# The first two token tiles of an MLP in k order, weight rows as they come, and a column sum by DMA transpose: one core of a Trainium2 chip

## The chip, the cores and the metric

The kernel runs on one core of a Trainium2 chip as one launch. The metric is the time of one execution on the device in microseconds (us); the median of the runs is compared. A profile of one execution shows when each instruction of each engine ran: TensorE (PE, with its weight loads PEld), VectorE (DVE), ScalarE (ACT), GpSimd (POOL) and the DMA queues that SyncE (SP) and ScalarE issue on.

## The reference

A linear-attention block and an MLP read the same layernormed input, and both are added to x. All tensors are bfloat16; the sequence has 2048 tokens, D = 640, F = 1536, and there are 32 heads of 20.

```python
xn = layernorm(x)                               # over D, eps 1e-5
# A: linear attention
q, k, v = split(xn @ wqkv)                      # 32 heads of 20
phi = lambda t: where(t > 0, t + 1, exp(t)) + 1e-6
pq, pk = phi(q), phi(k)
kv  = einsum("bhsd,bhse->bhde", pk, v)
z   = einsum("bhsd->bhd", pk)                   # the sum of pk over all tokens
num = einsum("bhqd,bhde->bhqe", pq, kv)
den = einsum("bhqd,bhd->bhq", pq, z)[..., None] + 1e-6
A = (num / den) @ wo
# B: the MLP
B = gelu(xn @ w1 + b1) @ w2 + b2
out = x + A + B
```

## The kernel before

Nothing is scheduled by a planner's costs: `Planner` only records what the program text calls for, one in-order list for each engine, and adds the semaphore waits that reads and writes of named resources need. The order on each engine is the order of the calls. An instruction group that ends in a mark increments its engine's semaphore once.

The 2048 tokens are 16 tiles of 128. x is loaded by tiles on SP's queue (`dma_x`), W1 in four quarters of 384 of its 1536 columns (`dma_w1`), between the loads of x: x0, x1, W1 quarters 0 and 1, x2, x3, quarter 2, x4 and x5, quarter 3, x6 and x7. x8 to x15 are issued later, in `ln_rest`. While the first data is under way, TensorE runs filler matmuls on constants.

A tile's layernorm is two `bn_stats` on VectorE (`ln_half`, halves of 320 columns), an aggregate, a power on GpSimd for the reciprocal deviation (`ln_aggr`), and one subtract and multiply on VectorE (`ln_norm`). The normalised tile must be transposed so that D lies on the partitions. Tiles 0 and 1 are transposed on TensorE into two PSUM banks (`transp2`, L331) and copied out by ScalarE (384 columns) and VectorE (256) in `copy2` (L339, L340); tile 2 on TensorE into one bank (`transp`, L374; `xnT_copy`, L382); all others by DMA transposes on SP's queue (`xnT_dma`, L263).

The first MLP matmul (`h_unit`, L393) takes one block of 128 of the 1536 hidden columns and n tiles of tokens: five matmuls, one for each 128 rows k of W1, sum in one PSUM bank, and ScalarE's GELU (L397) writes the result to HG. PSUM has 8 banks, handed out in a ring (`take`). A block needs its whole quarter of W1 and all five k of its tiles. The list `plan` sets TensorE's order: blocks of tile 0, `"T1"` (transposes of tile 1), more blocks of tiles 0 and 1 alone and together, `"T2"` (transposes of tile 2), then ever wider groups: 128, 256, 384 and at last 512 tokens a matmul.

After the MLP's first half come the keys (L502, L508, phi by ScalarE's exp at L490 and VectorE's L491 and L493), then G = xn^T pk (`g_group`, L535; `g_rem`, L544), while VectorE sums pk over the tokens (`z_sums`: 15 additions, L555 and L558, then a split into a high and a low bfloat16 part, L561 and L564). Then the queries (`q_chunk`, L588, with the same phi) in four chunks of five units. Between chunk 0 and chunk 1 stand `z_step` (L570: ten matmuls with a column of ones, one column each, which finish z; L574 copies it and L576 makes ZB) and `kvt_step` (L598, L605). The denominators (`den_mm`, L652) need ZB and all queries. The second MLP half and the attention's output (L709, L720) end the kernel. In the queues, SP carries every load, the DMA transposes and part of the stores; ScalarE's queue carries b1, the spread reciprocals and the other stores.

## Time and profile before

| | |
|---|---|
| median of 3 runs | 206.49 us (206.47 to 206.69) |
| the profiled execution: own time, span | 206.66 us, 204.9 us |
| TensorE busy | 201.3 us (98%), 1227 matmuls |
| VectorE, ScalarE, GpSimd busy | 108.2, 73.2, 34.0 us |
| first MLP matmul, first key matmul | 6.59 us, 59.65 us |
| moved by DMA | 21.37 MB, of it 13.08 MB read from HBM |

All times inside the profile count from the start of its span; the own time of that execution is longer by what lies around the span. A group's row gives the line, the engine, what it writes and reads, and how often; its length is that of one instruction alone, and matmuls are pipelined, so the distance between starts is shorter than the length. In the timeline, brackets give the idle time before an instruction and what ended it.

### The profile page before, as it was taken

The page shows a single profiled execution, that of the slowest core. Times are in us where ns is not written, and L with a number is a line of the kernel's source. Part 1 is how long each engine was busy: PE and PEld are TensorE (multiplying, and loading weights), DVE is VectorE, ACT ScalarE, POOL GpSimd, SP SyncE. Part 2 cuts the span into 40 slices and gives each one's busy share as a digit, 9 for nine tenths or more (in the row PEclk, how much of TensorE's full clock was granted, in tenths as well). Part 3 has the DMA queues.
Part 4 walks back from the last instruction along what each step waited for, and adds up shares of the span by engine and source line. Part 5 has one row for each costly group of instructions (what it writes and reads, how often), then busy time and mean ns, then how long its engine had stood idle before and what let it go on. Part 6 is the DMA issues. An engine that isn't in the chain of part 4 may idle for free.

```text
span 204.9 us, 3306 instructions
## 1 busy us (share of the span) xinstructions
PE 201.3 (98%) x1227; PEld 104.2 (51%) x1227; DVE 108.2 (53%) x236; ACT 73.2 (36%) x142; POOL 34.0 (17%) x85
## 2 busy tenths in 40 slices
PE   8999999999999999999999999999999999999995
...
GB/s 152 349 174 116 202 136 118 87 362 316 374 85 3 26 26 26 26 3 0 0 32 5 0 0 12 95 46 190 318 215 114 133 89 54 51 26 51 78 29 51
DMA packets 36217, 21.37 MB, mean 104 GB/s; under 512 B 21352, under 2 KB 36200, under 8 KB 36200
## 3 DMA queue, kind: packets, MB, share of 16 engines
...
q14 instruction: 7, 0.06, 0.1%
HBM read 13.08 MB, written 2.62 MB: 77 GB/s over the span
## 4 chain that ended last, share of the span: by engine, by line
PE 95%; DMA 3%; SPq 1%; DVE 0%; issue 0%
PE ps L709 29%; PE ps L393 25%; PE ps L588 11%; PE ps L502 8%; PE ps L535 8%; PE ps L720 7%; DMA W<-in_B_w_dram 3%; PE ps L544 2%; PE ps L508 2%; PE ps L642 1%; PE ps L598 1%; SPq L260 1%; PE ps L652 1%; DVE W L788 0%; PE ps L374 0%
## 5 line engine op out<-in xcount | busy, mean ns | idle before, releaser
L393 PE MATMUL ps<-xnT,W 128*128 128x128 bf16 (+3 forms) x405 | 52.7, 292 | 0.2
L397 ACT ACTIVATE HG<-ps,b1c 128x128 bf16<-128x128 f32 (+3 forms) x81 | 39.1, 514 | 14.6 <-PE ps L393 13.3
L709 PE MATMUL ps<-W,HG 128*128 128x512 bf16 (+2 forms) x204 | 43.9, 367 | 0.0
L393 PEld LDWEIGHTS ps<-xnT,W 128*128 128x128 bf16 x405 | 33.8, 98 | 18.5 <-DMA W<-in_B_w_dram 0.5
L709 PEld LDWEIGHTS ps<-W,HG 128*128 128x128 bf16 x204 | 19.5, 98 | 22.2 <-ACT Msb L624 0.2
L490 ACT ACTIVATE ek<-ps 128x512 bf16<-128x512 f32 x40 | 23.8, 597 | 19.4 <-PE ps L588 10.5
L491 DVE TENSOR_SCALAR ek<-ek 128x512 bf16<-128x512 bf16 x40 | 11.5, 288 | 29.1 <-ACT ek L490 29.1
L733 DVE TENSOR_TENSOR W<-ps,xnT 128x512 bf16<-128x512 f32 x15 | 10.4, 691 | 25.8 <-PE ps L709 19.3
L588 PE MATMUL ps<-xnT,Wqkv 128*128 128x512 bf16 x100 | 21.9, 379 | 0.0
L709 PE MATMUL ps<-Msb,PQ 128*128 128x512 bf16 (+2 forms) x85 | 19.6, 366 | 0.0
L344 DVE BATCH_NORM_STATS2 stats<-xPK 128x6 f32<-128x320 bf16 x32 | 14.0, 477 | 9.3 <-DMA xPK<-in_A_x_dram 9.3
L502 PE MATMUL ps<-Wqkv,xnT 128*128 128x512 bf16 x80 | 17.9, 379 | 0.0
L529 POOL COPY Wqkv<-Wqkv 128x128 bf16<-128x128 bf16 x25 | 14.0, 558 | 22.8 <-PE ps L508 21.3
L535 PE MATMUL ps<-xPK,xn_tm 128*128 128x512 bf16 x80 | 17.4, 379 | 0.0
L588 PEld LDWEIGHTS ps<-xnT,Wqkv 128*128 128x128 bf16 x100 | 9.7, 98 | 11.5
L493 DVE SCALAR_TENSOR_TENSOR PQ<-ps,ek 128x512 bf16<-128x512 f32 x20 | 13.8, 692 | 2.1
L709 PEld LDWEIGHTS ps<-Msb,PQ 128*128 128x128 bf16 x85 | 8.1, 98 | 9.2
L535 PEld LDWEIGHTS ps<-xPK,xn_tm 128*128 128x128 bf16 x80 | 7.8, 98 | 9.4
L502 PEld LDWEIGHTS ps<-Wqkv,xnT 128*128 128x128 bf16 x80 | 7.8, 98 | 9.4
L493 DVE SCALAR_TENSOR_TENSOR xPK<-ps,ek 128x512 bf16<-128x512 f32 x16 | 11.1, 692 | 1.7
L558 DVE TENSOR_TENSOR Msb<-Msb,xPK 128x640 f32<-128x640 f32 x14 | 11.6, 826 | 0.5
L354 POOL TENSOR_TENSOR rstd<-aggr,mhalf 128x1 f32<-128x1 f32 x16 | 9.9, 620 | 8.9 <-DVE aggr L352 8.9
...
## 6 DMA issues: line engine op xcount, KB each, us to landing
...
```

The source lines that it names most:

```text
L344: Pl.ins(v, lambda e: e.bn_stats(stats[:, s, 6 * h:6 * h + 6], x_in[:, t, h * HW:(h + 1) * HW]), reads=r_x[t], writes=[r_stats[s][h]])
L393: Pl.ins(pe, [(lambda e, k=k: e.matmul(bank(b, 0, w), W1[:, k, jb * P:(jb + 1) * P], xnT[:, k, tok], start=(k == 0), stop=(k == DT - 1))) ...
L397: Pl.ins(s_, lambda e: e.activation(HG[:, jb, tok], bank(b, 0, w), ACT.Gelu_apprx_tanh, bias=b1c[:, jb:jb + 1]), reads=[B_[b], r_b1c], wri ...
L490: Pl.ins(s_, lambda e: e.activation(e2, src, ACT.Exp), reads=br, writes=[r_ek[s]])
L493: Pl.ins(v, lambda e: e.scalar_tensor_tensor(out=d2, in0=src, scalar=0.0, in1=e2, op0=ALU.max, op1=ALU.add), reads=br + [r_ek[s]], writes= ...
L502: Pl.ins(pe, [(lambda e, k=k, b=b, t=t: e.matmul(bank(b), xnT[:, k, t * P:(t + 1) * P], Wqkv[:, k, D:D + MW], start=(k == 0), stop=(k == D ...
L529: Pl.ins(g, lambda e, k=k, i=i: e.tensor_copy(plain(Wqkv[:, k, D:2 * D], i), parts(Wqkv[:, k, 0:D], i)), reads=[r_Wq], writes=[r_Wk, r_WqP])
L535: Pl.ins(pe, lambda e, t=t, b=b, f=f, i=i: e.matmul(bank(b), xn_tm[:, t, f * P:(f + 1) * P], PK[:, t, 0:MW], start=(i == 0), stop=(i == NT ...
L558: Pl.ins(v, lambda e, t=t: e.tensor_tensor(out=zsum, in0=zsum, in1=PK[:, t, :], op=ALU.add), reads=[r_PK[t], r_PKr[t // CH], r_zsum], writ ...
L588: Pl.ins(pe, [(lambda e, k=k, j=j, b=b: e.matmul(bank(b), Wqkv[:, k, D + j * P:D + (j + 1) * P], xnT[:, k, cc], start=(k == 0), stop=(k == ...
L709: Pl.ins(pe, [(lambda e, i=i, x=x, bk=bk: e.matmul(bank(bk, 0, x[1] - x[0]), seq[i][0], seq[i][1][:, x[0]:x[1]], start=(i == 0), stop=(i = ...
L720: Pl.ins(pe, lambda e, i=i: e.matmul(bank(b), seq[i][0], seq[i][1], start=(i == 0), stop=(i == NS - 1)), reads=seq[i][2], writes=[B_[b]], ...
```

## The change

W1 arrives by its five rows k (128 of its 640 rows, all 1536 columns) instead of quarters of columns. Six PSUM banks are first set to zero by a matmul of ones with `pm`, a column of which half is 1 and half -1. The 12 blocks of tiles 0 and 1 then lie open in these six banks together, two blocks a bank, and TensorE goes through them k by k (`hk`); a block's GELU comes after its last k. x0 is loaded in two parts, 384 columns by SP's queue and 256 by ScalarE's, and its statistics follow these parts; its normalisation is split after the first 128 columns, and its transposes and copies go in three parts (`tr_part`, `cp_part`). Tiles 2 and 3 put four blocks of 128 tokens each into one bank (`h_pack`). Then tiles 4 and 5, and 6 and 7, go in pairs for nine blocks, and everything else 512 tokens wide. x8 to x11 are issued with the first loads. b1's transpose goes ahead of tile 0's. z is finished without TensorE and ahead of `g_group` in the program: one DMA transpose of the ten blocks of zhl on SP's queue, a reduction along the free axis and an addition on VectorE.

```diff
         zsum = Mf[:, 0:2 * D].bitcast(FP32)
...
+        zT = Mf[:, 0:2 * D].rearrange("p (a q) -> p a q", q=P)
         zhl = Mf[:, 2 * D:4 * D].rearrange("p (a d) -> p a d", a=2)
...
-        onesm = sb("onesm", [P, P], BF16)
+        pm = sb("pm", [P, 1], BF16)
...
+        z2 = sb("z2", [P, 2 * DT], FP32)
...
-        r_x = [[R_("x%d" % t)] for t in range(NT)]
+        r_x = [[R_("x%d_%d" % (t, i)) for i in range(2 if t == 0 else 1)] for t in range(NT)]
...
         r_xn = [[R_("xn%d_%d" % (t, i)) for i in range(2 if t == 0 else 1)] for t in range(NT)]
-        r_xnT = [[R_("xnT%d_%d" % (t, i)) for i in range(2 if t < 2 else 1)] for t in range(NT)]
-        W1P = [(i * F // 4, (i + 1) * F // 4) for i in range(4)]
-        r_W1 = [R_("W1_%d" % i) for i in range(len(W1P))]
+        r_xnT = [[R_("xnT%d_%d" % (t, i)) for i in range((3, 2)[t] if t < 2 else 1)] for t in range(NT)]
+        r_W1 = [R_("W1_%d" % k) for k in range(DT)]
...
         w1v = B_w1.rearrange("(k p) n -> p k n", p=P)
...
-        FW = [next(i for i, (lo, hi) in enumerate(W1P) if jb * P < hi) for jb in range(JT)]
...
             dma("sync", x_in[:, t:t + n, :], xv[t * P:(t + n) * P, :].rearrange("(t p) d -> p t d", p=P),
                 sum(r_x[t:t + n], []))
-        def dma_w1(i):
-            lo, hi = W1P[i]
-            dma("sync", W1[:, :, lo:hi], w1v[:, :, lo:hi], [r_W1[i]])
-
-        dma_x(0, 1)
+        def dma_w1(k):
+            dma("sync", W1[:, k, :], w1v[:, k, :], [r_W1[k]])
+
+        XA = 3 * P
+        for i, (lo, hi) in enumerate(((0, XA), (XA, D))):
+            dma(("sync", s_)[i], x_in[:, 0, lo:hi], xv[0:P, lo:hi], [r_x[0][i]])
         dma_x(1, 1)
         dma_w1(0)
         dma_w1(1)
+        dma_w1(2)
         dma_x(2, 1)
+        dma_w1(3)
         dma_x(3, 1)
-        dma_w1(2)
+        dma_w1(4)
         dma_x(4, 2)
-        dma_w1(3)
         dma_x(6, 2)
-
-        Pl.ins(g, lambda e: e.memset(onesm[:], 1.0), writes=[r_ones])
+        dma_x(8, 2)
+        dma_x(10, 2)
+
+        Pl.ins(v, lambda e: e.memset(pm[0:P // 2], 1.0), writes=[r_pm])
+        Pl.ins(v, lambda e: e.memset(pm[P // 2:P], -1.0), writes=[r_pm])
         Pl.ins(g, lambda e: e.memset(mhalf[:], -0.5), writes=[r_small])
         Pl.ins(g, lambda e: e.memset(ident[:], 0.0), writes=[r_ident])
         Pl.ins(g, lambda e: e.affine_select(out=ident[:], in_=ident[:], compare_op=ALU.not_equal,
...
                                            nc.const_aps.tensor(1.0, [P, w], BF16), start=True, stop=True)
                         for _ in range(n)], writes=[B_[b]])
-        def b1_step():
-            b = take(1)
-            Pl.ins(pe, lambda e: e.transpose(bank(b).bitcast(BF16)[:, 0:JT], b1tmp[:], ident[:JT, :JT]),
-                   reads=[r_b1tmp, r_ident], writes=[B_[b]])
-            Pl.ins(s_, lambda e: e.activation(b1c[:], bank(b).bitcast(BF16)[:, 0:JT], ACT.Copy),
-                   reads=[B_[b]], writes=[r_b1c])
-
-        XA = 3 * P
-
-        def transp2(t, b0, b1):
-            for lo, hi, b in ((0, 3, b0), (3, DT, b1)):
-                pT = bank(b).bitcast(BF16)
-                Pl.ins(pe, [(lambda e, k=k, pT=pT, lo=lo: e.transpose(
-                    pT[:, (k - lo) * P:(k - lo + 1) * P], xn_tm[:, t, k * P:(k + 1) * P], ident[:]))
-                    for k in range(lo, hi)], reads=[r_xn[t][0 if lo == 0 else -1], r_ident], writes=[B_[b]])
-
-        def copy2(t, b0, b1):
+        b1T = bank(6).bitcast(BF16)[:, 2 * P:2 * P + JT]
+
+        def b1_pe():
+            Pl.ins(pe, lambda e: e.transpose(b1T, b1tmp[:], ident[:JT, :JT]),
+                   reads=[r_b1tmp, r_ident], writes=[B_[6]])
+
+        def b1_copy():
+            Pl.ins(s_, lambda e: e.activation(b1c[:], b1T, ACT.Copy), reads=[B_[6]], writes=[r_b1c])
+
+        PARTS = [((6, 0, 1, s_), (7, 1, 3, s_), (7, 3, DT, s_)), ((6, 0, 3, s_), (7, 3, DT, v))]
+
+        def xT(t, k):
+            return r_xnT[t][next(i for i, (_, lo, hi, _) in enumerate(PARTS[t]) if lo <= k < hi)]
+
+        def tr_part(t, i):
+            b, lo, hi, _ = PARTS[t][i]
+            pT = bank(b).bitcast(BF16)
+            Pl.ins(pe, [(lambda e, k=k: e.transpose(
+                pT[:, k * P:(k + 1) * P], xn_tm[:, t, k * P:(k + 1) * P], ident[:]))
+                for k in range(lo, hi)], reads=[r_xn[t][min(i, len(r_xn[t]) - 1)], r_ident], writes=[B_[b]])
+
+        def cp_part(t, i):
+            b, lo, hi, eng = PARTS[t][i]
             tok = slice(t * P, (t + 1) * P)
-            pA = bank(b0).bitcast(BF16)[:, 0:XA].rearrange("p (k q) -> p k q", q=P)
-            pB = bank(b1).bitcast(BF16)[:, 0:D - XA].rearrange("p (k q) -> p k q", q=P)
-            Pl.ins(s_, lambda e: e.activation(xnT[:, 0:3, tok], pA, ACT.Copy), reads=[B_[b0]], writes=[r_xnT[t][0]])
-            Pl.ins(v, lambda e: e.tensor_copy(xnT[:, 3:DT, tok], pB), reads=[B_[b1]], writes=[r_xnT[t][1]])
+            src = bank(b).bitcast(BF16)[:, lo * P:hi * P].rearrange("p (k q) -> p k q", q=P)
+            Pl.ins(eng, lambda e: e.activation(xnT[:, lo:hi, tok], src, ACT.Copy) if eng == s_ else
+                   e.tensor_copy(xnT[:, lo:hi, tok], src), reads=[B_[b]], writes=[r_xnT[t][i]])
         def ln_half(t, h):
             s = t % 4
-            Pl.ins(v, lambda e: e.bn_stats(stats[:, s, 6 * h:6 * h + 6], x_in[:, t, h * HW:(h + 1) * HW]),
-                   reads=r_x[t], writes=[r_stats[s][h]])
+            cut = XA if t == 0 else HW
+            lo, hi = ((0, cut), (cut, D))[h]
+            Pl.ins(v, lambda e: e.bn_stats(stats[:, s, 6 * h:6 * h + 6], x_in[:, t, lo:hi]),
+                   reads=[r_x[t][min(h, len(r_x[t]) - 1)]], writes=[r_stats[s][h]])
             if h == 0:
                 Pl.ins(g, lambda e: e.tensor_single_scalar(stats[:, s, 2:3], stats[:, s, 2:3], D * EPS, ALU.add),
                        reads=[r_stats[s][0]], writes=[r_stats[s][0]])
...
             ln_half(t, 1)
             ln_aggr(t)
-        def ln_norm(t):
+        def ln_norm(t, part=None):
             s = t % 4
             for i, r in enumerate(r_xn[t]):
-                lo, hi = (0, D) if len(r_xn[t]) == 1 else ((0, XA), (XA, D))[i]
+                if part not in (None, i):
+                    continue
+                lo, hi = (0, D) if len(r_xn[t]) == 1 else ((0, P), (P, D))[i]
                 Pl.ins(v, lambda e, lo=lo, hi=hi: e.tensor_scalar(
                     xn_tm[:, t, lo:hi], x_in[:, t, lo:hi], aggr[:, s, 0:1], rstd[:, t:t + 1],
                     ALU.subtract, ALU.mult),
...
             Pl.ins(pe, [(lambda e, k=k: e.matmul(
                 bank(b, 0, w), W1[:, k, jb * P:(jb + 1) * P], xnT[:, k, tok],
                 start=(k == 0), stop=(k == DT - 1))) for k in range(DT)],
-                reads=[r_W1[FW[jb]]] + sum(r_xnT[t0:t0 + n], []), writes=[B_[b]])
+                reads=r_W1 + sum(r_xnT[t0:t0 + n], []), writes=[B_[b]])
             Pl.ins(s_, lambda e: e.activation(
                 HG[:, jb, tok], bank(b, 0, w), ACT.Gelu_apprx_tanh, bias=b1c[:, jb:jb + 1]),
                 reads=[B_[b], r_b1c], writes=[r_HG[t][jb] for t in range(t0, t0 + n)])
...
                writes=[r_b1c])
         dma(s_, b1tmp[:], B_b1.rearrange("(a p) -> a p", p=P), [r_b1tmp])
-        filler(10)
-        filler(6, P)
+        def h_pack(t, j0):
+            b = take(1)
+            tok = slice(t * P, (t + 1) * P)
+            Pl.ins(pe, [(lambda e, k=k, i=i: e.matmul(
+                bank(b, i * P, i * P + P), W1[:, k, (j0 + i) * P:(j0 + i + 1) * P], xnT[:, k, tok],
+                start=(k == 0), stop=(k == DT - 1))) for i in range(4) for k in range(DT)],
+                reads=r_W1 + r_xnT[t], writes=[B_[b]])
+            for i in range(4):
+                Pl.ins(s_, lambda e, i=i: e.activation(
+                    HG[:, j0 + i, tok], bank(b, i * P, i * P + P), ACT.Gelu_apprx_tanh, bias=b1c[:, j0 + i:j0 + i + 1]),
+                    reads=[B_[b], r_b1c], writes=[r_HG[t][j0 + i]])
+
+        def at(b):
+            ring[0] = b
+
+        def hk(t, n, jb, ks):
+            b = jb // 2
+            o = (jb % 2) * 2 * P + t * P
+            tok = slice(t * P, (t + n) * P)
+            Pl.ins(pe, [(lambda e, k=k: e.matmul(
+                bank(b, o, o + n * P), W1[:, k, jb * P:(jb + 1) * P], xnT[:, k, tok],
+                start=False, stop=(jb % 2 == 1 and k == DT - 1))) for k in ks],
+                reads=[r_W1[k] for k in ks] + [xT(u, k) for u in range(t, t + n) for k in ks],
+                writes=[B_[b]])
+            if DT - 1 in ks and jb % 2:
+                for i in range(2):
+                    Pl.ins(s_, lambda e, i=i, jb=jb - 1 + i: e.activation(
+                        HG[:, jb, tok], bank(b, i * n * P, (i + 1) * n * P), ACT.Gelu_apprx_tanh, bias=b1c[:, jb:jb + 1]),
+                        reads=[B_[b], r_b1c], writes=[r_HG[u][jb - 1 + i] for u in range(t, t + n)])
+
+        at(6)
+        filler(3)
+        for b in range(6):
+            Pl.ins(pe, lambda e, b=b: e.matmul(
+                bank(b), nc.const_aps.tensor(1.0, [P, P], BF16), pm[:].broadcast_to((P, 512)), start=True, stop=False),
+                reads=[r_pm], writes=[B_[b]])
+        at(7)
+        filler(5, P)
+        at(7)
         ln_half(0, 0)
         ln_half(0, 1)
         ln_aggr(0)
         ln_half(1, 0)
         ln_half(1, 1)
-        ln_norm(0)
-        b = take(2)
-        transp2(0, b, b + 1)
+        ln_norm(0, 0)
         ln_aggr(1)
-        copy2(0, b, b + 1)
-        b1_step()
-        filler(3, P)
+        ln_norm(0, 1)
         ln_norm(1)
+        b1_pe()
+        tr_part(0, 0)
+        cp_part(0, 0)
+        b1_copy()
+        filler(2, P)
+        tr_part(0, 1)
+        tr_part(0, 2)
+        cp_part(0, 1)
+        cp_part(0, 2)
         h_list = lambda t, n, lo, hi: [(t, n, jb) for jb in range(lo, hi)]
-        plan = h_list(0, 1, 0, 3) + ["T1"] + h_list(0, 1, 3, 6) + h_list(1, 1, 0, 6)
-        plan += h_list(0, 2, 6, 7) + ["T2"] + h_list(0, 2, 7, 9) + h_list(2, 1, 0, 9) + h_list(0, 3, 9, JT)
-        plan += h_list(3, 1, 0, 3) + h_list(4, 1, 0, 3) + h_list(3, 2, 3, JT) + h_list(5, 3, 0, JT)
-        plan += h_list(8, 2, 0, 3) + h_list(10, 2, 0, 3) + h_list(8, 4, 3, JT) + h_list(12, 4, 0, JT)
+        k_list = lambda t, n, ks, lo=0, hi=JT: [(t, n, jb, ks) for jb in range(lo, hi)]
+        pack = lambda t, lo, hi: [(t, jb) for jb in range(lo, hi, 4)]
+        plan = k_list(0, 1, [0]) + ["T1"] + k_list(0, 1, [1]) + k_list(1, 1, [0]) + k_list(1, 1, [1])
+        plan += k_list(0, 2, [2]) + k_list(0, 2, [3], 0, 8) + ["T2"]
+        plan += k_list(0, 2, [4], 0, 8) + k_list(0, 2, [3, 4], 8)
+        plan += pack(2, 0, JT) + pack(3, 0, JT) + h_list(4, 2, 0, 9) + h_list(6, 2, 0, 9)
+        plan += h_list(4, 4, 9, JT) + h_list(8, 4, 0, JT) + h_list(12, 4, 0, JT)
         def ln_rest():
             def out(t):
...
             ln_stats(7)
             out(6)
             out(7)
-            dma_x(8, 2)
-            dma_x(10, 2)
             dma_x(12, 4)
             ln_stats(8)
             for t in range(8, NT):
...
         for u in plan:
             if u == "T1":
-                b = take(2)
-                transp2(1, b, b + 1)
-                copy2(1, b, b + 1)
+                for i in range(2):
+                    tr_part(1, i)
+                    cp_part(1, i)
                 ln_stats(2)
                 ln_half(3, 0)
                 ln_half(3, 1)
                 ln_norm(2)
                 ln_aggr(3)
-                ln_half(4, 0)
             elif u == "T2":
+                at(7)
                 b = transp(2)
-                xnT_copy(2, b)
                 ln_norm(3)
                 xnT_dma(3)
-                ln_half(4, 1)
-                ln_aggr(4)
+                xnT_copy(2, b)
+                ln_stats(4)
                 ln_rest()
+            elif len(u) == 2:
+                h_pack(*u)
+            elif len(u) == 4:
+                hk(*u)
             else:
                 h_unit(*u)
         run_masks(len(mask_jobs))
...
                        reads=[r_zsum, r_zhl], writes=[r_zhl])
         def z_step():
-            b = take(1)
-            Pl.ins(pe, [(lambda e, j=j, i=i: e.matmul(bank(b, j, j + 1), zhl[:, i, j * P:(j + 1) * P], onesm[:, 0:1],
-                                                      start=(i == 0), stop=(i == 1)))
-                        for j in range(DT) for i in range(2)],
-                   reads=[r_zhl, r_ones], writes=[B_[b]])
-            Pl.ins(v, lambda e: e.tensor_copy(z_sb[:], bank(b, 0, DT)), reads=[B_[b]], writes=[r_z])
+            dma_t("sync", zT, Mf[:, 2 * D:4 * D], [r_zT, r_zsum], reads=[r_zhl])
+            Pl.ins(v, lambda e: e.tensor_reduce(out=z2[:], in_=zT, axis=mybir.AxisListType.X, op=ALU.add), reads=[r_zT], writes=[r_z2])
+            Pl.ins(v, lambda e: e.tensor_tensor(out=z_sb[:], in0=z2[:, 0:DT], in1=z2[:, DT:2 * DT], op=ALU.add),
+                   reads=[r_z2], writes=[r_z])
             for j in range(DT):
                 Pl.ins(v, lambda e, j=j: e.tensor_scalar(ZB[:, j, :], hmask[:, j // 2, :], z_sb[:, j:j + 1], None, ALU.mult),
                        reads=[r_z, r_hmask], writes=[r_ZB])
         z_sums()
+        z_step()
         for f in range(DT):
             g_group(f)
         g_rem()
...
                    reads=[r_xr[t // CH], r_b2], writes=[r_xb[t]])
         q_chunk(0)
-        z_step()
         kvt_step()
         q_chunk(1)
         q_chunk(2)
```

## The prediction

> **What bounds the kernel now.** I read the page first (shares of the engines), then the chain of work that ended last in order of time, then the timeline of the first 26 us and of 96 to 132 us, and last the DMA issues.
>
> ```profile
> PE 201.3 (98%) x1227; PEld 104.2 (51%) x1227; DVE 108.2 (53%) x236; ACT 73.2 (36%) x142; POOL 34.0 (17%) x85
> PE 95%; DMA 3%; SPq 1%; DVE 0%; issue 0%
> ```
>
> TensorE bounds everything. The pieces of the chain say where it does not:
>
> ```profile
> 2.20 5.74 DMA W<-in_B_w_dram
> ...
> 7.98 3.23 PE ps L393 x50
> 11.21 0.28 PE ps L374 x5
> 11.49 48.32 PE ps L393 x340
> ...
> 81.39 17.27 PE ps L535 x80
> ...
> 108.40 0.23 PE ps L570 x10
> ```
>
> From 7.98 us on there is only TensorE, back to back. So time can be won in two ways alone: TensorE's useful work starts earlier, or it gets less work; and it is lost wherever a new wait appears. The small matmuls for z (L570) are 0.23 us of the chain. The start, in the timeline (start, length, engine, what; idle time before it in brackets):
>
> ```profile
> 3.17 0.89 DVE L344 BATCH_NORM_STATS2 stats<-xPK 128x6 f32<-128x320 bf16 x2 [3.17 <-DMA xPK<-in_A_x_dram]
> 5.13 0.64 DVE L366 TENSOR_SCALAR xn_tm<-xPK,aggr,rstd 128x384 bf16<-128x384 bf16 x2
> 5.57 0.54 PE L331 MATMUL ps<-ident,xn_tm 128*128 128x128 bf16 x5 [0.27 <-DVE xn_tm L366]
> 6.57 0.84 PEld L393 LDWEIGHTS ps<-xnT,W 128*128 128x128 bf16 x15 [0.25 <-DMA W<-in_B_w_dram]
> 6.59 1.00 PE L393 MATMUL ps<-xnT,W 128*128 128x128 bf16 x15
> 7.98 2.96 PEld L393 LDWEIGHTS ps<-xnT,W 128*128 128x128 bf16 x50 [0.29 <-DMA W<-in_B_w_dram]
> ```
>
> Tile 0 could have been multiplied from about 6.4, but the first quarter of W1 ends the wait at 6.57 and the second at 7.98. Behind both stands the layernorm of x0, which lets nothing useful begin before 5.57.
>
> **The change, part by part.** Starts of back-to-back matmuls of 128, 256, 384 and 512 columns lie 56, 109, 162.5 and 216 ns apart in the trace (15 of 128 in 1.00 us with one lasting 219 ns; 5 of 512 in 1.08 us).
>
> *Amount of MLP work.* Before: 135, 90, 75 and 105 of the four widths = 7.56 + 9.81 + 12.19 + 22.68 = 52.24 us. After: 168, 126, 0 and 135 = 9.41 + 13.73 + 29.16 = 52.30. With ten transposes for tiles 1 and 2 (0.56) that is 52.80 and 52.86: 0.06 us more. The next stage's first matmul started at 59.65, so before behaves as if it had begun at 59.65 - 52.80 = 6.85 and never paused. The 24 more weight loads hide: PEld is half idle.
>
> Now 80 groups end in a semaphore increment each where a block of five matmuls had one. The trace: L535 gives 80 matmuls an increment each and takes 17.27 us, 216 ns each, as the groups of five do. The Trainium skill ("TensorE: Matmul & The Clock Gate", The cost: per-tile semaphore tail) says against this change that increments serialize at 26.3 ns each; laid on top of the matmuls that is 80 x 26.3 = 2.1 us, and the change would lose 1.2 us. But 26 ns fits into the 56 ns of the narrowest group as into 216, so I take 0 and keep the rule in the upper tail.
>
> *When useful work starts.* x0 lands so that its statistics start at 3.17. Its first 384 columns are 60% of the bytes: 96 of 160 KB at the 348 GB/s that the windows show for 5.57 to 7.98 save at most 0.19 us, if the rest does not share the wires. The skill ("DMA: Bandwidth & Descriptors", Issuing engines are not separate DMA queues) speaks against it: transfers of both queues interleave on the same engines, and a second queue saves issue time alone; by it this gain is nothing and the sum below 0.70. I take 0.15, since ACT's first transfer before was issued 0.07 later than SP's and took longer to issue (0.63 against 0.40): 3.02. The rest is needed 0.45 later. The sums are of the same 640 columns (0.89), and aggregate, rstd (0.57 on POOL) and tile 1's two statistics follow in the old order, so the first normalisation moves from 5.13 to 4.98. It is now 128 columns (384 took 0.38 and 256 0.34: about 0.30), then tile 1's aggregate, then 512 columns (0.42) to 5.75. The four transposes run 5.81 to 6.04; block 0's copy on ScalarE (between the 0.17 of the b1 copy and the 0.49 of 384 columns, say 0.27) is done at 5.87 beneath them. First useful matmul: 6.05.
>
> Ahead of that, six matmuls that zero the banks stand in for fillers (9 wide ones and 5 narrow, ending about 4.85 where 10 and 6 ended at 5.14): both sets end before the first transpose, so they cost nothing, and TensorE is kept as busy for its clock. Their two memsets run on VectorE at 0.8, idle until 3.0. b1's transpose now stands first in TensorE's queue; its 3 KB are issued on ACT's queue one issue (0.63) later than at 0.87 and wanted at 4.9; x0's whole transfer took 2.3 us, so about 3.8.
>
> Row 0 of W1 must be there. x1 landed at 3.64; 393 KB at 348 GB/s give 4.8, at the pace of the old first quarter (491 KB from 3.64 to 6.53) 5.95. Either way in time.
>
> Twelve matmuls (0.67) bring 6.72. Tile 1's normalisation waits for rstd (6.07) and ends at 6.63; its second transposes wait until ScalarE has emptied bank 7 of two copies of 256 columns (0.39 each, from 6.26, overlapping by 0.1: 6.94). That is a new stall of 0.12. Effective start 6.17, against 6.85: 0.68 less 0.06 = 0.62 us won.
>
> *Covers behind it.* Row 1 is needed at 7.13, row 2 at 9.14, row 3 at 10.45, row 4 at 11.60. At 348 GB/s with x2 and x3 between, they land at 5.9, 7.1, 8.7 and 10.3, and x3 at 9.15; then two statistics (0.95) and tile 2's normalisation (0.45) end near 10.65, before its transposes at 11.3. ScalarE has no GELU until 12.0, then 12 of 256 columns (steps 0.38) and 24 of 128 (0.28) to 23.3. TensorE meets bank 0 at 13.34 (emptied 12.8), fills a bank in 20 x 56 = 1.12 us where ScalarE frees one in 0.76, and returns to bank 5 near 23.9 (free 23.3). No stall, 0.6 to spare. On VectorE tile 3's normalisation now goes ahead of tile 2's copy out of the bank, which must wait for TensorE until 11.8 anyway and ends at 12.3, wanted at 13.34. SP now issues x8 and x10 before tile 3's transpose (13 issues of 0.4 to 1.6 us, over by about 9); those 1.3 MB after row 4 end near 13.9, so that transpose (2.6 issue to landing, asked for at 11.8) lands by 15.5, needed at 16.7. Tiles 4 and 5 follow as before (18.7, needed 20). The POOL queue only loses a memset.
>
> *z.* TensorE loses ten matmuls: 0.23. VectorE gets the work, ahead of phi for the first queries:
>
> ```profile
> 99.92 1.60 DVE L564 TENSOR_TENSOR Msb<-Msb 128x128 bf16<-128x128 f32 x5
> 104.75 0.29 DVE L491 TENSOR_SCALAR ek<-ek 128x512 bf16<-128x512 bf16 x1 [3.23 <-ACT ek L490]
> 127.34 0.69 DVE L493 SCALAR_TENSOR_TENSOR PQ<-ps,ek 128x512 bf16<-128x512 f32 x1
> 128.79 1.26 PE L652 MATMUL ps<-PQ,ZB 128*32 128x512 bf16 x20
> ```
>
> ```profile
> xPK<-Msb SPq DMA_TRANSPOSE x4, 2.4
> W<-Msb SPq DMA_TRANSPOSE x1, 2.6
> ```
>
> Four blocks land in 2.4 us, five in 2.6; ten, at 0.15 a block, in 3.3 (from below 2.6, from above twice a five: 5.2). So z starts at 101.54 on SP's empty queue and lands at 104.84. A reduction of 1280 elements, scaled from statistics of 320 in 0.44 to 0.48: 1.47. Then the add 0.15 and five ZB (1.31): phi of unit 0 starts at 107.8 instead of 104.75, 3.0 late. VectorE needs 1.00 us a unit against TensorE's 1.08 and no longer does z's 1.4 us between units 4 and 5, so unit 5 starts at 113.9 against 112.67, and unit 19 ends 14 x 1.0 + 1.1 later at 129.0 (it was 128.03). Behind it waits only the last fifth of the den matmuls, which start at 128.79 - 0.23 and reach it at 129.4: 0.4 to spare. Bank 0 is wanted again at 110.7 and free at 108.9; POOL's KVP is 1.3 late with 14 us to spare; the transpose of the last G row is asked for at 103.97, when SP has issued z's (1.2 to 2.4 long). I cost it at nothing and gain 0.23.
>
> *Sum.* 0.62 + 0.23 = 0.85. The profiled run: span 204.9, own time 206.66, so 1.76 lies around the span; 204.05 + 1.76 = 205.81. The median before is 0.17 below that run: 205.64, say 205.6.
>
> **Rivals.** (1) *z comes late* (slower). The place is den behind unit 19, the cover 0.4 us. If ten blocks cost twice five (5.2), z is 1.9 late, den waits 1.5, and 0.85 turns into a loss of 0.65: 207.1. It decides for slower from 4.55 us of transpose (3.3 + 0.4 + 0.85). For it: no ten-block transpose is in the trace. Against: the step from four to five. (2) *The rows come late.* x3 now stands behind four rows (1573 KB of W1) instead of two quarters. If the slow beginning of the old first quarter (170 GB/s) repeats, everything lands 1.2 later, tile 2's transposes wait 0.6 and row 4 little: about 206.2. Against: each row is 128 pieces of 3 KB instead of 640 of 768 bytes. (3) *The start does not move*: no gain from x0's parts, b1's transpose late on ACT's queue behind x0, copies slower; useful start 6.45, about 206.0. (4) *Better*: x0 a full 0.2 earlier, no bank stall: 205.3.
>
> **How the numbers follow.** Forecast with (4): 0.66. Rival 3: 0.12, two thirds of it still faster by over 0.2% (0.41 us, about what a measurement of this kernel can tell from no change; the line is 206.08). Rival 2: 0.11, two thirds within. Rival 1: 0.11, nearly all slower. That makes 0.78 faster, 0.12 same, 0.10 slower. Range 205.1 (rival 4 and a little) to 206.4: rival 1 beyond its point is left out.
>
> **What would show it.** Right: first row-wise matmul near 6.05, no wait for W1 anywhere before 60, the next stage's first matmul near 59.0, L570 gone and den starting without a gap. Wrong: the first useful matmul at 6.4 or later; idle time of TensorE ended by W1, by VectorE's tile 2 or by GELU; a z transpose of over 4 us; gaps over 56 ns among the row-wise matmuls; TensorE idle before or inside den.

## The result and the profile after

Over six runs of each, the changed kernel took 206.03 us (205.93 to 206.18) and the kernel before 206.69 us (206.47 to 206.74): a ratio of 0.9971, with a 95% interval of 0.9958 to 0.9984. That is 0.66 us faster, where 0.85 us was forecast. The profiled execution of the changed kernel has an own time of 206.18 us and a span of 204.5 us, against 206.66 and 204.9.

First the page of the changed kernel: the engines' busy shares, and the shares of the chain of work that ended last.

```profile
PE 200.7 (98%) x1238; PEld 104.6 (51%) x1238; DVE 108.8 (53%) x238; ACT 71.3 (35%) x144; POOL 33.5 (16%) x84
PE 96%; DMA 2%; SPq 0%; DVE 0%; issue 0%
```

TensorE is still the bound. The same chain in order of time (start, length, what):

```profile
1.73 4.59 DMA W<-in_B_w_dram
6.32 0.05 issue
6.37 0.84 PE ps L439 x12
7.21 0.28 PE ps L342 x5
7.49 4.22 PE ps L439 x56
...
13.73 6.70 PE ps L423 x120
...
80.99 17.27 PE ps L596 x80
...
128.21 1.26 PE ps L712 x20
```

The chain still begins with a load of W1, now row 0 (L261), which ends at 6.32 and releases the first row-wise matmul (L439) at 6.37. The 120 matmuls of 128 columns for tiles 2 and 3 (L423) take 6.70 us: 56 ns each. L570 is gone. The timeline shows what stood ready when row 0 came (start, length, engine, what; in brackets the idle time before it and what ended it):

```profile
3.06 0.89 DVE L357 BATCH_NORM_STATS2 stats<-xPK 128x6 f32<-128x384 bf16 x2 [2.01 <-DMA xPK<-in_A_x_dram]
5.04 0.31 DVE L381 TENSOR_SCALAR xn_tm<-xPK,aggr,rstd 128x128 bf16<-128x128 bf16 x1
5.38 0.36 DVE L381 TENSOR_SCALAR xn_tm<-xPK,aggr,rstd 128x512 bf16<-128x512 bf16 x1
5.67 0.28 ACT L350 ACTIVATE xnT<-ps 128x128 bf16<-128x128 bf16 x1 [2.92 <-PE ps L342]
5.80 0.40 PE L342 MATMUL ps<-ident,xn_tm 128*128 128x128 bf16 x4
6.36 0.67 PEld L439 LDWEIGHTS ps<-xnT,W 128*128 128x128 bf16 x12 [0.34 <-DMA W<-in_B_w_dram]
```

The layernorm of x0 ran as forecast, block 0 was copied out at 5.95, and from then on TensorE waited for W1. From 6.37 to den it is never idle. In the middle of the kernel, z on VectorE:

```profile
101.54 1.33 SPq L264 DMA_TRANSPOSE Msb<-Msb  x1
104.89 1.49 DVE L631 TENSOR_REDUCE z<-Msb 128x10 f32<-128x1280 bf16 x1 [3.37 <-DMA Msb<-Msb]
106.61 1.31 DVE L635 TENSOR_SCALAR ZB<-hmask,z_sb 128x32 bf16<-128x32 bf16 x5
107.83 0.29 DVE L552 TENSOR_SCALAR ek<-ek 128x512 bf16<-128x512 bf16 x1
...
128.32 0.69 DVE L554 SCALAR_TENSOR_TENSOR PQ<-ps,ek 128x512 bf16<-128x512 f32 x1
...
129.07 0.10 PEld L712 LDWEIGHTS ps<-PQ,ZB 128*32 128x32 bf16 x4 [0.38 <-DVE b2c L754]
...
129.40 1.81 PE L702 MATMUL ps<-Wo,W 128*32 128x320 bf16 x48
```

Each length and each start up to phi's first unit is where the forecast put it. But den's last four matmuls (L712) waited: VectorE's last unit of phi, the instruction ahead of the b2c that is named as the releaser, ended at 129.02, where the next den matmul was due. That delay of 0.05 us, together with a slower step into the next group (0.33 us from den's last fifth to L702, where 0.21 is the regular step), gave back about 0.19 us.

Two differences hold the result. The first key matmul began at 59.24 instead of 59.65: the start won 0.41, not 0.62. From the first key matmul to the end of the last matmul it is 142.92 us instead of 142.98: z won 0.25 and den lost 0.19. The sum is 0.47; the own times differ by 0.48. This execution was the slowest of the six. Between the medians it is 0.66, and how those divide between start and den, no trace says.

### The profile page after: what moved, and what is told of

Same layout as the page of the kernel before. It is cut to its first block, busy times and chain, and to the rows that moved or that the text cites. A ratio compares the mean times of both kernels' runs of the same rounds, so it can differ in the third digit from the quotient of the medians.

```text
span 204.5 us, 3358 instructions
## 1 busy us (share of the span) xinstructions
PE 200.7 (98%) x1238; PEld 104.6 (51%) x1238; DVE 108.8 (53%) x238; ACT 71.3 (35%) x144; POOL 33.5 (16%) x84
## 3 DMA queue, kind: packets, MB, share of 16 engines
q10 hardware_dynamic: 4056, 3.61, 6.6%
## 4 chain that ended last, share of the span: by engine, by line
PE 96%; DMA 2%; SPq 0%; DVE 0%; issue 0%
PE ps L768 29%; PE ps L408 19%; PE ps L648 11%; PE ps L596 8%; PE ps L563 8%; PE ps L779 7%; PE ps L439 3%; PE ps L423 3%; DMA W<-in_B_w_dram 2%; PE ps L605 2%; PE ps L569 2%; PE ps L702 1%; PE ps L658 1%; PE ps L712 1%; SPq L261 0%; DVE W L847 0%
## 5 line engine op out<-in xcount | busy, mean ns | idle before, releaser
L408 PE MATMUL ps<-xnT,W 128*128 128x512 bf16 (+1 forms) x225 | 39.1, 336 | 0.0
L408 PEld LDWEIGHTS ps<-xnT,W 128*128 128x128 bf16 x225 | 21.9, 98 | 16.8 <-issue 0.3
L412 ACT ACTIVATE HG<-ps,b1c 128x512 bf16<-128x512 f32 (+1 forms) x45 | 26.3, 670 | 11.3 <-PE ps L408 10.8
L590 POOL COPY Wqkv<-Wqkv 128x128 bf16<-128x128 bf16 x25 | 13.5, 540 | 22.4 <-PE ps L569 20.9
L357 DVE BATCH_NORM_STATS2 stats<-xPK 128x6 f32<-128x320 bf16 (+2 forms) x32 | 13.9, 478 | 5.3 <-DMA xPK<-in_A_x_dram 5.3
```

Of the source, the lines that this page charges most:

```text
L357: Pl.ins(v, lambda e: e.bn_stats(stats[:, s, 6 * h:6 * h + 6], x_in[:, t, lo:hi]), reads=[r_x[t][min(h, len(r_x[t]) - 1)]], writes=[r_stat ...
L408: Pl.ins(pe, [(lambda e, k=k: e.matmul(bank(b, 0, w), W1[:, k, jb * P:(jb + 1) * P], xnT[:, k, tok], start=(k == 0), stop=(k == DT - 1))) ...
L412: Pl.ins(s_, lambda e: e.activation(HG[:, jb, tok], bank(b, 0, w), ACT.Gelu_apprx_tanh, bias=b1c[:, jb:jb + 1]), reads=[B_[b], r_b1c], wri ...
L590: Pl.ins(g, lambda e, k=k, i=i: e.tensor_copy(plain(Wqkv[:, k, D:2 * D], i), parts(Wqkv[:, k, 0:D], i)), reads=[r_Wq], writes=[r_Wk, r_WqP])
```

## The experiments

Twelve experiments ran in three series; two of them (after_again and zb_again) run a kernel once more. Medians of different series are compared with the kernel before in their own series (206.57, 206.73 and 206.67 us). "Row 0" is when its last byte had landed, "start" the first useful MLP matmul, "keys" the first key matmul, "rest" the time from there to the end of the last matmul, all from the profiled execution of each. That execution was often among the longest of its kernel, so a profile shows mechanisms, and the median what they are worth. The ratio is estimated from all runs; where some are long (z_only, touch, w1act, shift, zb_shift) it lies nearer to 1 than the quotient of the two medians.

| kernel | median, range (runs) | ratio, 95% interval | row 0 | start | keys | rest |
|---|---|---|---|---|---|---|
| before (first profile) | 206.69 | 1 | quarter: 6.53 | 6.59 | 59.65 | 142.98 |
| changed (first profile) | 206.03, 205.93 to 206.18 (6) | 0.9971, 0.9958 to 0.9984 | 6.32 | 6.37 | 59.24 | 142.92 |
| z_only | 206.44, 206.37 to 207.66 (13) | 0.9998, 0.9987 to 1.0009 | | 6.86 | 59.77 | 142.73 |
| start_only | 206.23, 206.00 to 206.56 (21) | 0.9982, 0.9975 to 0.9988 | 5.49 | 6.50 | 59.54 | 142.98 |
| zb_pool | 205.89, 205.78 to 206.17 (5) | 0.9967, 0.9955 to 0.9979 | 6.38 | 6.43 | 59.27 | 142.73 |
| touch | 206.24, 205.87 to 208.91 (14) | 0.9993, 0.9974 to 1.0012 | 7.62 | 7.66 | 62.13 | 142.75 |
| after_again | 206.12, 205.75 to 207.08 (22) | 0.9974, 0.9966 to 0.9982 | 6.78 | 6.83 | 59.69 | 143.37 |
| row0_half | 206.81, 206.18 to 207.36 (14) | 1.0002, 0.9992 to 1.0013 | 5.80 | 6.18 | 59.85 | 142.88 |
| w1act | 206.49, 206.14 to 208.38 (14) | 1.0000, 0.9981 to 1.0019 | 5.59 | 6.25 | 59.40 | 142.79 |
| x0_whole | 206.22, 205.93 to 206.45 (7) | 0.9976, 0.9965 to 0.9986 | 6.80 | 6.85 | 59.69 | 142.73 |
| shift | 206.02, 205.79 to 207.60 (22) | 0.9983, 0.9968 to 0.9998 | 6.64 | 6.69 | 59.57 | 142.73 |
| row0_less | 206.09, 205.77 to 206.52 (22) | 0.9969, 0.9961 to 0.9977 | half: 6.16 | 6.21 | 59.41 | 142.82 |
| zb_shift | 206.85, 205.81 to 207.96 (22) | 1.0000, 0.9985 to 1.0015 | 6.46 | 6.51 | 60.58 | 142.73 |
| zb_again | 205.84, 205.80 to 206.32 (10) | 0.9959, 0.9945 to 0.9972 | 5.60 | 6.11 | 59.04 | 142.74 |

### z_only and start_only: the two halves of the change, each alone

z_only is the kernel before with z_step as changed and called ahead of the G groups; start_only is the changed kernel with z finished on TensorE between chunks 0 and 1, as before:

```diff
-            dma_t("sync", zT, Mf[:, 2 * D:4 * D], [r_zT, r_zsum], reads=[r_zhl])
-            Pl.ins(v, lambda e: e.tensor_reduce(out=z2[:], in_=zT, axis=mybir.AxisListType.X, op=ALU.add), reads=[r_zT], writes=[r_z2])
...
+            b = take(1)
+            Pl.ins(pe, [(lambda e, j=j, i=i: e.matmul(bank(b, j, j + 1), zhl[:, i, j * P:(j + 1) * P], onesm[:, 0:1],
+                                                      start=(i == 0), stop=(i == 1)))
...
         z_sums()
-        z_step()
...
         q_chunk(0)
+        z_step()
         kvt_step()
```

> The kernel before with the new z alone. Theory (the gains add and the loss comes from their meeting): TensorE loses 0.23 us of matmuls, unit 19 of phi ends near 129.0 and the last fifth of den reaches it at 129.4, so den runs without a gap and the span falls by 0.23 (median about 206.4 to 206.5 beside 206.7). Rival (z on VectorE holds den up by itself): an idle stretch of TensorE of 0.1 to 0.2 us ended by VectorE inside den, and a span within 0.1 of before.

> The changed kernel with z back on TensorE in its old place. Theory: the start is worth 0.40 us (first key matmul near 59.25 instead of 59.65), den runs without a gap, span 0.40 below before, so about 0.07 longer than the whole change (median about 206.3). Rival (the loss inside den has to do with the start, not with z): the gap at den stays and the span is only 0.2 below before.

In z_only the rest is 142.73, 0.25 less than before: ten matmuls gone, and no wait in den, where all 20 matmuls stood in one piece. So the transpose, the reduction and the ZB on VectorE cost nothing in that place. The median fell by 0.13 us, which its interval doesn't tell from nothing. start_only's rest is 142.98, as before, and its median fell by 0.34 us, with an interval clear of 1. The two medians add up to 0.47, less than the whole change's 0.66 and 0.61 (after_again). But z_only's interval alone is 0.45 us wide, so that the medians neither show nor exclude that the halves add.

start_only's own profile shows a second thing that the forecast did not count. Row 0 was there at 5.49, but TensorE began at 6.50. Until then TensorE's matmuls of 128 columns stood 107 ns apart instead of 56, and x1 had come late, at 4.52:

```profile
5.70 0.29 PE L344 MATMUL ps<-ident,xn_tm 128*128 128x128 bf16 x1 [0.21 <-DVE xn_tm L383]
5.78 0.42 PE L323 MATMUL ps<-const-bfloat16-1.0 128*128 128x128 bf16 x2
6.10 0.61 PE L344 MATMUL ps<-ident,xn_tm 128*128 128x128 bf16 x4
6.50 0.95 PE L441 MATMUL ps<-xnT,W 128*128 128x128 bf16 x12
```

The four transposes that take 0.61 us here take 0.40 in the changed kernel's profile. The trace's record of the full granted clock begins at 4.24 us in the changed kernel's first profile and at 6.72 here; over all profiles the step from 107 to 56 ns lies between about 4.2 and 6.8 us. How much of the late start is the pace and how much x1, this run does not separate.

### after_again: the changed kernel once more

> The changed kernel once more, for a second profile. Theory (the 0.17 us lost at den in the first profile came from one slow DMA transpose of key sums at 82.8, which made z_sums start 26.47 us after the first key matmul instead of 26.06): here z_sums starts at 26.06, unit 19 ends 0.4 earlier against TensorE and den runs without a gap, so last matmul minus first key matmul is 142.73 and not 142.92. Rival (z's lag on VectorE always reaches den): the gap inside den is there again and the difference is 142.9.

The median is 206.12, a ratio of 0.9974. In its profile den waited longer than in the first, 0.50 us, and the rest is 143.37: the loss at den is no accident of one execution. Its start won nothing: row 0 came at 6.78 and the first key matmul at 59.69, where that of before came at 59.65. It is the longest of its 22 runs, so what made the median 0.61 us shorter than before is not to be read from it. What both profiles share is the view of the DMA transposes of the keys (L264) between 76 and 92 us: shortest, median and longest issue in ns, first and last start. The changed kernel, first profile:

```profile
L264 SPq DMA_TRANSPOSE xPK<-Msb x2: 1189/1445/1701, 77.4 to 82.8; - x2
```

The changed kernel, second profile:

```profile
L264 SPq DMA_TRANSPOSE xPK<-Msb x2: 1189/1542/1896, 77.8 to 83.2; - x2
```

The kernel before, same view (L263 there):

```profile
L263 SPq DMA_TRANSPOSE xPK<-Msb x2: 1189/1190/1190, 77.8 to 83.2; - x2
```

The second of these transposes brings the last keys that the sums over tokens wait for, and it took 0.5 and 0.7 us longer to issue. z_sums then began 26.47 and 26.65 us after the first key matmul instead of 26.06, and all of VectorE's list behind it was late: sums, z, ZB and phi.

What a late phi costs can be read across the profiles. Where its last unit ended 0.25 to 0.40 us ahead of the den matmul that needs it (touch, z_only, x0_whole, shift), the rest is 142.73 to 142.75. At 0.12, 0.09, 0.03 and 0.00 us ahead (w1act, row0_less, row0_half, the changed kernel's first) it is 142.79, 142.82, 142.88 and 142.92, and at 0.45 us too late (after_again) 143.37. So the loss begins some 0.2 us before phi is late: the step from den to L702 grows from 0.21 to 0.33 us, while den itself hardly waits. Why it grows, no run shows.

### zb_pool and zb_again: ZB on GpSimd, so that phi can start 1.3 us earlier

```diff
             for j in range(DT):
-                Pl.ins(v, lambda e, j=j: e.tensor_scalar(ZB[:, j, :], hmask[:, j // 2, :], z_sb[:, j:j + 1], None, ALU.mult),
+                Pl.ins(g, lambda e, j=j: e.tensor_scalar(ZB[:, j, :], hmask[:, j // 2, :], z_sb[:, j:j + 1], None, ALU.mult),
                        reads=[r_z, r_hmask], writes=[r_ZB])
```

> The changed kernel with the five products for ZB on GpSimd instead of VectorE. Theory: phi of the first queries starts about 1.3 us earlier (106.5 instead of 107.8), unit 19 ends near 127.8, den no longer waits for VectorE and the 0.17 us between 128 and 131 come back: median 0.15 to 0.2 below the whole change. Rival (den's wait isn't VectorE's lag, or ZB on GpSimd comes too late): no change, or TensorE waiting for GpSimd before den.

> The changed kernel with its five ZB on GpSimd, once more, on the chip of the other three. Theory: den does not wait even if the transpose before the sums is issued slowly (any issue up to 1.9), first key matmul to the end of the last matmul 142.73, median 0.1 to 0.2 below the changed kernel's 206.03 to 206.12, ratio 0.996 to 0.997. Rival (its better median in the first series came from the few runs): ratio 0.9975 as the changed kernel.

In both, phi's last unit ends at 127.4, 1.6 and 1.5 us ahead of its use; den does not wait, and the rest is 142.73 and 142.74. In the profile of zb_again the transpose of the keys took 1.43 us to issue, and that no longer mattered. The ratios are 0.9967 and 0.9959, the best of all kernels; zb_again lies 0.83 us below the kernel before. Its interval overlaps that of the changed kernel, so the gain over the changed kernel, 0.02 to 0.22 us by medians set against their own series, is shown by the traces rather than by the times.

zb_again's is also the one profile of the kernels with these loads in which nothing held up the start: row 0 came in time, at 5.60, and so did x1 (3.61) and TensorE's full pace. Its chain of waits begins differently:

```profile
0.79 2.27 DMA xPK<-in_A_x_dram
...
3.08 0.90 DVE stats L357 x2
...
5.48 0.29 DVE xn_tm L381
...
5.82 0.40 PE ps L342 x4
6.21 0.73 PE ps L439 x12
6.94 0.38 PE ps L342 x5
```

No piece of W1 is left in it. The matmuls start at 6.11 and the keys at 59.04, so that the start behaves as if it had begun at 59.04 - 52.86 = 6.18 us. That is the forecast's 6.17. Its last matmul ended at 201.78 us, where that of before ended at 202.63: 0.85 us. This execution, 205.80 us, was the fastest of its ten.

### touch: two columns of row 0 read early

The idea was that the slow first reads of W1 are paid once by each DMA engine, and that a tiny load ahead could pay them.

```diff
         dma_x(1, 1)
+        tch = sb("tch", [P, 2], BF16)
+        dma(s_, tch[:], w1v[:, 0, 0:2], [R_("tch")])
         dma_w1(0)
```

> The changed kernel with one small extra load on ScalarE's queue, two elements of each of the 128 pieces of row 0 of W1 into an unused tile, ahead of everything but x0. Theory (the first read of W1 by each DMA engine is what costs 0.3 to 1.1 us): the small load pays these first reads, row 0 lands near 5.2 instead of 6.32, the first row-wise matmul starts near 6.05 instead of 6.37, and the median falls by about 0.3 below the whole change. Rival (row 0 is late by the amount that is queued, or any early traffic pays such reads): row 0 lands at 6.3 as before or later, and the median does not fall.

Row 0 came at 7.62, and nothing supports the idea. But the tiny load itself landed only at 3.82, with row 0's stream already under way, so it tries the idea from there on alone: of the 20 packets that took 0.32 to 0.86 us between 2.6 and 5.0 us, nine began after it. The load also delayed b1, whose transpose (L330) stands first in TensorE's list:

```profile
6.66 0.18 PE L330 MATMUL ps<-ident,b1tmp 12*128 12x12 bf16 x1 [1.32 <-DMA b1tmp<-in_B_b_dram]
```

From 8.59 us on TensorE's granted clock was 0.5 for 3.4 us, and this execution took 208.91 us. b1's place at the head of TensorE's list is a risk that the forecast named and that no other profile met.

### row0_half, row0_less, w1act and x0_whole: what makes row 0 late

row0_half loads row 0 as two halves with a wait of its own for each. row0_less goes further, and loads the first half alone; the other half is set to zero, so that this kernel leaves a tenth of W1 out:

```diff
-            dma("sync", W1[:, k, :], w1v[:, k, :], [r_W1[k]])
+            if k:
+                dma("sync", W1[:, k, :], w1v[:, k, :], [r_W1[k]])
+                return
+            dma("sync", W1[:, 0, 0:F // 2], w1v[:, 0, 0:F // 2], [r_W1[0]])
+            Pl.ins(g, lambda e: e.memset(W1[:, 0, F // 2:F], 0.0), writes=[r_W1[DT]])
...
```

> The changed kernel with row 0 of W1 loaded as two halves of its columns, so that the first six matmuls need only 196 KB. Theory (layernorm would allow the first row-wise matmul at 6.05 and only row 0's last bytes hold it to 6.37): the first half lands near 5.9, the first matmul starts at 6.05 to 6.1 and the end moves by 0.2 to 0.3; median 0.2 to 0.3 lower. Rival (a few DMA engines stall in their first reads of the stream, whatever the size of the piece): the first half lands near 6.2 too, and nothing moves by more than 0.1.

> The changed kernel with half of row 0 of W1 (196 KB) left out: set to zero by GpSimd instead of loaded, so its output is not the reference's. It prices the lateness of the first rows. Theory (bytes of the first rows set the start): the first row-wise matmul comes at 6.05 to 6.2 with no wait for row 0, row 1 lands by 6.7 and is not waited for, and the first key matmul comes at 58.95 to 59.1 instead of 59.24 to 59.69; the median falls by 0.3 to 0.5. Rival 1 (the stream lags whatever its bytes): the half row comes at 6.3 or later, and nothing changes. Rival 2 (half the row lets it start, but row 1 still lands at 7.3 or later): start 6.1, then a wait of over 0.3 for row 1, and the first key matmul at 59.2 to 59.4 as before.

In row0_half the halves landed at 5.26 and 5.80 and the matmuls started at 6.18, but row 1 came at 7.91, where it came at 7.29 and 7.75 in the changed kernel's two profiles, and the wait stood there:

```profile
6.18 0.83 PE L443 MATMUL ps<-xnT,W 128*128 128x128 bf16 x12
...
7.95 0.23 PE L443 MATMUL ps<-xnT,W 128*128 128x128 bf16 x1 [0.58 <-DMA W<-in_B_w_dram]
```

Nothing was won: 206.81 us. row0_less has 196 KB fewer to bring, and yet its half of row 0 landed at 6.16 and row 1 at 7.48, not by 6.7. Its median, 206.09, is that of the changed kernel. So fewer bytes alone do not bring the first rows earlier. (Its profile is not clean: TensorE worked at 107 ns a matmul until 6.7 us, so its keys at 59.41 do not say what the rows alone would give.) What the DMA records show in all these profiles is the beginning of the stream: between 2.6 and 5.0 us 16 (w1act) to 28 (zb_again) of the packets took 0.3 to 1.7 us each instead of about 0.1. A load has landed only when the slowest of its 16 DMA engines is done: row 0's engines finished between 4.66 and 6.32 us in the changed kernel's first profile, between 4.58 and 5.60 in zb_again. That it is these packets which make an engine late is argued, since the records do not name a packet's engine, and their number does not tell: zb_again has the most of them. Why they are slow is open.

All engines together were not slow. A window from x1's landing to that of row 0 gives the busy times of the engines and, at the end of the line, TensorE's clock, the DMA engines' busy share and the GB/s that they moved. The changed kernel, first profile:

```profile
3.64:6.32 2.68, 2.10 (x16) 1.02 (x14) 2.02 (x8) 0.44 (x3) 1.62 (x4) 1.00 0.98 352
```

zb_again:

```profile
3.61:5.60 1.99, 1.94 (x12) 1.02 (x10) 1.86 (x8) 0.00 (x0) 1.06 (x4) 1.00 0.94 323
```

The kernel before, to the landing of its first quarter:

```profile
3.64:6.53 2.89, 2.59 (x19) 1.28 (x17) 2.42 (x9) 0.56 (x2) 1.55 (x4) 1.00 0.97 313
```

In the changed kernel's first profile 14 of row 0's 16 engines were done by 5.55 us, and twelve had finished row 1 as well by 6.27. Row 0 waited for the last two, at 6.16 and 6.32.

w1act issues row 0 on ScalarE's queue ahead of b1, and so moves b1's transpose back to where tile 2 is transposed; x0_whole loads x0 in one transfer.

```diff
-            dma("sync", W1[:, k, :], w1v[:, k, :], [r_W1[k]])
+            dma(s_ if k == 0 else "sync", W1[:, k, :], w1v[:, k, :], [r_W1[k]])
...
-        b1_pe()
...
-        b1_copy()
...
             elif u == "T2":
+                b1_pe()
+                b1_copy()
                 at(7)
```

```diff
-        for i, (lo, hi) in enumerate(((0, XA), (XA, D))):
-            dma(("sync", s_)[i], x_in[:, 0, lo:hi], xv[0:P, lo:hi], [r_x[0][i]])
+        dma_x(0, 1)
```

> The changed kernel with row 0 of W1 issued on ScalarE's queue right behind the second part of x0 (at 1.25 instead of 1.73), and b1's transpose and copy moved to the place of tile 2's transposes, since b1's load then comes after that row. Theory (row 0 is late because it is issued third): it lands 0.4 earlier, near 5.9, and the first row-wise matmul starts at 6.05 to 6.1. Rival (it now shares the engines with x1): x1 lands 0.3 to 0.5 later, tile 1's statistics hold the first normalisation on VectorE, and the first row-wise matmul starts no earlier than 6.3.

> The changed kernel with x0 loaded whole on SP's queue. Theory (row 0 of W1 sets the start, so x0's two parts are worth nothing): statistics start at 3.17 instead of 3.06, and the first row-wise matmul stays at 6.3 to 6.4 and the median within 0.1 of the whole change. Rival (layernorm sets the start): both move 0.1 later.

In w1act row 0 came at 5.59, but x1 only at 4.38 instead of 3.64, and the late transpose of b1 cost TensorE two gaps of 0.1 us; the start was 6.25 and the median 206.49. x0_whole shows that the two parts of x0 are worth little: its statistics began at 3.15 instead of 3.06, and its row 0 came at 6.80, as late as in after_again. Its median, 206.22, lies 0.1 above the changed kernel's in the same series, as the rival had it, but 0.1 is within what the runs of one kernel differ by.

### shift and zb_shift: what slows the transpose of the keys

The trace also records the packets by which the chip fetches instructions ("q8 instruction" on the page: ten packets of 16 KB). One of them falls near 83 us in the changed kernel and at 88 us in the kernel before. Set against the issue of the transpose, in us from the issue's start:

| profile | packet ends | issue takes | difference |
|---|---|---|---|
| before, z_only | none near | 1.19 | |
| zb_pool | 0.64 | 1.19 | |
| start_only | 0.74 | 1.19 | |
| x0_whole | 0.87 | 1.29 | 0.42 |
| touch | 0.90 | 1.33 | 0.43 |
| w1act | 1.02 | 1.43 | 0.41 |
| zb_again | 1.04 | 1.43 | 0.39 |
| row0_less | 1.09 | 1.52 | 0.43 |
| row0_half | 1.13 | 1.54 | 0.41 |
| changed, first profile | 1.27 | 1.70 | 0.43 |
| changed, second profile | 1.46 | 1.90 | 0.44 |

From a packet end of about 0.8 us on, the issue ends 0.39 to 0.44 us after the packet. To make this more than a coincidence, shift puts more instructions into TensorE's list, ahead of everything useful, so that its packets come earlier; zb_shift is the same with ZB on GpSimd.

```diff
         at(6)
-        filler(3)
+        filler(2)
+        at(6)
+        filler(5, P)
```

> The changed kernel with one of the three first wide fillers replaced by five narrow ones: four matmuls and eight instructions more in TensorE's list before anything useful, about 0.1 us longer among idle filler time. Theory (an instruction packet meets the transpose): in six profiles the DMA transpose issued 0.8 us after the last keys takes 1.19 us when the 16 KB packet of the instruction queue near it has ended within 0.76 us of the issue's start, and otherwise until 0.43 us after that packet's end (1.29, 1.43, 1.54, 1.70, 1.90). The packets come about 26 us apart, as TensorE goes through 256 instructions, so eight more instructions bring the one near 83 us about 0.9 us earlier, before the transpose. Then the transpose is issued in 1.19, the sums over tokens start 26.06 after the first key matmul, den does not wait, and first key matmul to the end of the last matmul is 142.73 (142.92 in the changed kernel's first profile, 143.37 in its second). The median falls by up to 0.2 us against the changed kernel's 206.03 to 206.12. Rival (the transpose is slow for another reason, such as the time at which it falls): issue again 1.4 to 1.9, sums at 26.3 to 26.7, den waits.

> Both mends together, as a candidate that beats both kernels: the changed kernel with its five ZB on GpSimd and with the eight early instructions more. Theory: with ZB off VectorE den has 1.5 us of cover, so that the slower transpose no longer reaches it; the shift then adds nothing, and the median is that of the kernel with ZB on GpSimd alone within 0.1 us, near 205.9; first key matmul to last matmul's end 142.73. Rival (something else between keys and den also costs): still under 142.6 here.

The packet came at 81.39 in shift and at 82.18 in zb_shift, 1.7 and 1.9 us ahead of the transpose: it moved by about 2 us against the transpose, twice as far as I had worked out. Shift's transposes of the keys:

```profile
L264 SPq DMA_TRANSPOSE xPK<-Msb x2: 1190/1190/1190, 77.7 to 83.1; - x2
```

Back at 1.19; z_sums began 26.05 after the first key matmul, den did not wait although ZB is on VectorE, and the rest is 142.73. So the packet is the cause of the loss at den.

zb_shift, though, is slower than zb_pool, and its profile has a hole in TensorE that no other profile has:

```profile
21.62 0.82 PE L408 MATMUL ps<-xnT,W 128*128 128x256 bf16 x6 [1.06 <-DMA xnT<-xn_tm]
```

Two matmuls lie 1.28 us apart there, 1.2 us lost, and the view of the transposes of tiles 4 and 5 in zb_shift says why:

```profile
L264 SPq DMA_TRANSPOSE xnT<-xn_tm x2: 1199/1200/1202, 15.7 to 17.1; - x2
...
PE ps L408: 1.1, 1
...
DMA to landing us min/median/max: 2.6/3.5/4.3
```

Tile 5's transpose, issued at 17.15, landed 4.3 us later instead of 2.6. The packet of instructions near 19 us began 2.12 us after that issue, while the transpose was still under way. In the changed kernel it began 2.36 us after, and tile 5 landed at 19.62 as it should; there tile 6, behind it, took 4.4 us, which nothing waited for. In six more profiles the packet began 2.33 to 2.37 us after that issue, and tile 5 landed after 2.6. The hole is thus a quarter of a microsecond away; what sets the distance no run shows. In 7 of shift's 22 runs the time is 207.0 to 207.6 us, some 1.2 above the others, and in 13 of zb_shift's it is above 206.7. That these have the same hole is likely, but those runs left no trace; nor does a run show by itself that the fillers brought it on. So shift mends den and yet is no better kernel; ZB on GpSimd mends it with no such hole in its two profiles.

## Why the prediction was right, and where its sum was off

*TensorE bounds, and the gain is an earlier start and less work.* Right: in the first profile 0.41 from the start and 0.25 from z, less 0.19. These make 0.47, and the medians 0.66; the profiled executions were mostly among the longest, so how late row 0 is in an ordinary one stays open. The range, 205.1 to 206.4, had room for both losses.

*Amount of MLP work, 0.06 us more.* Right: in the five profiles where the start waited for row 0 and nothing followed (both of the changed kernel, zb_pool, x0_whole, shift) the first key matmul came 52.84 to 52.88 us after the first row-wise one, and 52.86 was forecast. The increments cost nothing: in the chain above, 56 row-wise matmuls with one increment each (36 of 128 columns, 20 of 256) took 4.22 us, and 56 and 109 ns apart they make 4.20. The Trainium skill's serial 26.3 ns for each increment ("TensorE: Matmul & The Clock Gate", The cost: per-tile semaphore tail), a fit to small tiles packed side by side, gave an estimate of 2.1 us for the 80; the trace decides against adding it here.

*x0 in two parts, 0.15 us.* Nearly: 3.06 against 3.17 before and 3.15 in x0_whole, so 0.09 to 0.11, where the rule that the forecast held against it gave nothing.

*The layernorm chain, useful start 6.05, stall 0.12.* Right: 5.04 and 5.38 for the normalisations against 4.98 and 5.3, block 0 out at 5.95 to 5.97, start 6.11 in zb_again, where bank 7 then cost 0.08.

*"Row 0 of W1 must be there ... 4.8 ... 5.95. Either way in time."* This is the term that was mis-sized. In the seven profiles of kernels with the same loads, row 0 landed at 6.32, 6.78, 6.38, 6.64 and 6.46 us (first and second profile of the changed kernel, zb_pool, shift, zb_shift) and in time only twice, at 5.49 and 5.60 (start_only, zb_again). The forecast divided row 0's bytes by a rate. Its rate was right: 348 GB/s, and the engines moved 352 from x1's landing to row 0's. But a load lands with its slowest engine, and the last two of 16 finished row 0 at 6.16 and 6.32 us, while others were already done with row 1. The slow end, 170 GB/s, was no pace of the engines either: they moved 313 while the old first quarter came. In the first profile this was worth 0.21 us (59.24 instead of about 59.03). The pieces of 3 KB, which I had held against a late row, did not prevent it. The rival "the rows come late" thus was half of what happened: late by 0.3 to 0.7 against the 6.05 at row 0, not at tile 2 or row 4. Its 206.2, and the 206.0 of the rival "the start does not move", were worked from a median before of 206.49: gains of 0.29 and 0.49. The result gained 0.66 on the 206.69 beside it, and so lies between these two and the forecast's 0.85. Of the 0.43 us between 206.03 and the forecast's 205.6, 0.20 is that difference of the two medians before. Which execution has its row 0 at 5.49 and which at 6.78 is chance as far as these runs show.

*z, 0.23 us, and its chain on VectorE.* Right in every length: ten blocks landed after 3.32 us against 3.3 (3.55 in the second profile), reduction 1.49 against 1.47, ZB 1.31. The starts agree to 0.06 us for a reason the forecast did not have: it left the sums where they were before, and although the start had won 0.41, the slow transpose had lost them 0.41. And z_only, zb_pool, zb_again, x0_whole and shift all show 142.73 or 142.74.

*"0.4 to spare" at den.* Right as a number: with z_sums at 26.06 and ZB on VectorE, x0_whole's phi ended 0.37 us ahead of its use. The failed step is "I cost it at nothing": the 0.4 held only if the sums began as long after the keys as before, and the packet took 0.4 to 0.6 of it; and of the 0.4 only about half was free, since the loss begins at 0.2. The rival "z comes late" named the right place and the wrong cause: the ten blocks took 3.32 us, as forecast, and the delay came in 19 us earlier, at the transpose of the keys.

With ZB on GpSimd, and in an execution in which row 0 was in time, the sum came out: 0.85 in zb_again's trace, and 0.83 between its median and that of before. Row 0's lateness is not mended by this: zb_pool, with the same kernel, met it at 6.38.
